# Eleven warm-up matmuls instead of nine ahead of an attention kernel

## The chip, the cores and the metric

The kernel runs on one core of a Trainium2 chip. The metric is the device time of one execution in microseconds (us), as the median of several executions. The profile of an execution also gives its span, from the first to the last instruction; it is 1.7 to 2.0 us shorter than the time. A change counts as faster or slower from 2% on.

## The reference

Two attention blocks read the same x (2048 tokens, 1024 features, bf16, 32 heads of 32) and are mixed by a gate:

```python
g = sigmoid((x * gate_w).sum(-1, keepdims=True))
a = linear_attention(x, A_wqkv) @ A_wo            # phi(q) (phi(k)^T v) / (phi(q) sum phi(k))
b = local_attention(x, B_wqkv, W=8, dil=2) @ B_wo # each token sees 8 keys, two apart
return g * a + (1 - g) * b
```

Nearly all of the work is dense matmuls of 128 x 128 weights on 512 columns.

## The kernel before

The kernel records operations with priorities, and a small list scheduler orders them for each engine. These parts matter here. The zeros of the warm-up, and the warm-up itself, which writes a bank of PSUM (the memory that takes the results of matmuls) that nobody reads:

```python
C("dve", lambda e: e.memset(warm[:, :], 0.0), 0.15, [warm.all()])
for m in mx[0:2]:
    C("dve", lambda e, m=m: e.memset(m[:, :], 0.0), 0.2, [m.all()])
...
for i in range(WARM):
    P.op("pe", lambda e: e.matmul(banks[7].ap(), warm[:, 0:128], warm[:, :], start=True, stop=True), 0.43,
         reads=[warm.all()], writes=[banks[7].iv], prio=-1)
```

The first loads: x tile 0 and half of the first weights in four pieces, then more x tiles, then the other half of the weights, again in four pieces:

```python
load_x(0, 0)                                   # tile, priority
load_w(0, 0, Bw, 2048, 0.1, 0, 2, "act")       # two pieces from the queue of ScalarE
load_w(0, 0, Bw, 2048, 0.2, 2, 4, "act")
load_w(0, 0, Bw, 2048, 0.3, 4, 6)              # two from the queue of SyncE
load_w(0, 0, Bw, 2048, 0.4, 6, 8)
for t in range(1, NT):
    load_x(t, 3 + t)
for d in range(0, 8, 2):
    load_w(0, 1, Bw, 2560, 6.1 + 0.1 * d, d, d + 2)
```

TensorE then works in groups of eight matmuls: x tiles 0 to 3 on the first half of the weights, the same tiles on the second half, then tiles 4 to 7, and so on. The result of a group is then copied out of PSUM by another engine; I call this copy its eviction. Much later in the program, in the last third, a sum over each chunk of 512 tokens is taken by matmuls on `zsel` (L1598 in the profile). This part was not changed, but it comes up below:

```python
for n, (u, j) in enumerate(nums):
    numer(u, j)
    if j == 7:
        after(3, lambda u=u: over(u))     # over(u) issues the L1598 matmuls three slots later
    slot(0)
    ...
```

## Time and profile before

| | before |
|---|---|
| time, median of 3 | 491.82 us (491.49 to 493.79) |
| span of the profiled execution | 492.6 us |
| TensorE busy | 478.7 us, 97% |
| warm-up matmuls | 1.25 to 5.27 us |
| idle until the first tile of x has landed | 1.20 us |
| first real matmul | 6.47 us |

The profiled execution took 494.49 us, longer than each of the three that were timed. The prediction rests on it.

From the page of the profile before: its busy table and its chain of waits (the chain is followed back from the last instruction; shares are of the span).

```profile
PE 478.7 (97%) x5055; PEld 226.9 (46%) x5121; DVE 274.4 (56%) x487; ACT 166.9 (34%) x287; POOL 5.0 (1%) x27
...
PE 91%; DMA 3%; DVE 2%; issue 2%; SPq 1%; ACT 1%; ACTq 0%
```

TensorE (PE) bounds the kernel, so time saved on TensorE reaches the end unless TensorE then waits.

The timeline of TensorE before, first 10 us: start, length, engine, line, operation, tiles, count, and in brackets the idle time ahead of it and what ended that.

```profile
1.25 4.02 PE L1365 MATMUL ps_all<-warm 128*128 128x512 bf16 x9 [1.25 <-DVE warm L1279]
6.47 3.92 PE L1326 MATMUL ps_all<-w,xT 128*128 128x512 bf16 x9 [1.20 <-DMA xT<-in_A_x_dram]
```

Read the lengths: nine warm-up matmuls take 4.02 us and nine real ones 3.92 us, about 440 ns each. Single records start every 427 ns in both rows; from 10.2 us on they start every 216 ns. So the first real matmuls run at half the clock. The trace holds a record of the granted clock as well: full from 10.17 us. (The clock row of the page shows full speed from the start, since it knows nothing before the first record. The spacing of the matmuls is what to trust.)

What TensorE waited for over the whole span before: total us, times, longest.

```profile
PE ps_all L1326 <- issue: 6.0, 38, 0.2
PE ps_all L1365 <- DVE warm L1279: 1.2, 1, 1.2
PE ps_all L1326 <- DMA xT<-in_A_x_dram: 1.2, 1, 1.2
PE ps_all L1598 <- DVE xT L1339: 0.7, 1, 0.7
PE ps_all L1326 <- ACT kT L1358: 0.2, 1, 0.2
```

The 6.0 us of "issue" are holes where the trace lost a matmul record (38 of the 66 that are missing; each hole is one matmul long), not waits.

### The profile page before, as it was taken

What the parts mean: (1) busy time and instruction counts of PE and PEld (TensorE: products, weight loads), DVE (VectorE), ACT (ScalarE), POOL (GpSimd) and SP (SyncE); (2) the same over time, 40 slices, a digit from 0 to 9 for tenths busy, and PEclk for the clock granted to TensorE, in tenths of its full rate; (3) what the DMA queues carried; (4) which work ended last, traced back from release to release, by engine and by line L of the source; (5) the groups of instructions that cost most, each with busy time, mean ns of one, the idle gap of its engine ahead of it and who ended that gap; (6) DMA issues with size and microseconds to landing.
All of it is one profiled execution on the core that took longest, in us unless ns stands there. A gap on an engine that the chain in (4) does not pass through costs nothing.

```text
span 492.6 us, 11357 instructions
## 1 busy us (share of the span) xinstructions
PE 478.7 (97%) x5055; PEld 226.9 (46%) x5121; DVE 274.4 (56%) x487; ACT 166.9 (34%) x287; POOL 5.0 (1%) x27
## 2 busy tenths in 40 slices
PE   8999999999999999999999999999999999999997
PEld 2444444444444444555454454444444444444443
DVE  2121435889777777465555645596865735334434
ACT  1211111222344344665655556355423223010000
POOL 3000000000000000000000000000000000000000
PEclk9999999999999999999999999999999999999999
DMA  8999993232013036201000100501673407101212
GB/s 212 214 201 305 318 358 100 73 95 90 3 27 115 24 116 156 65 26 44 24 24 24 36 12 4 170 3 25 168 191 74 122 11 182 44 23 45 85 67 89
DMA packets 51069, 48.82 MB, mean 99 GB/s; under 512 B 20161, under 2 KB 38977, under 8 KB 51010
## 3 DMA queue, kind: packets, MB, share of 16 engines
q1 hardware_dynamic: 50322, 47.40, 34.6%
q8 instruction: 42, 0.69, 0.6%
q10 hardware_dynamic: 688, 0.59, 0.4%
q14 instruction: 17, 0.14, 0.1%
HBM read 34.34 MB, written 9.44 MB: 89 GB/s over the span
## 4 chain that ended last, share of the span: by engine, by line
PE 91%; DMA 3%; DVE 2%; issue 2%; SPq 1%; ACT 1%; ACTq 0%
PE ps_all L1326 74%; PE ps_all L1647 11%; PE ps_all L1418 2%; PE ps_all L1437 2%; DMA rb<-rc_hbm 1%; DMA xT<-in_A_x_dram 1%; PE ps_all L1519 1%; SPq L1611 1%; PE ps_all L1444 1%; DMA rc_hbm<-ra 1%; DVE zsel L1561 1%; DVE pq L1339 0%; PE ps_all L1598 0%; PE ps_all L1571 0%; DVE e L1337 0%
## 5 line engine op out<-in xcount | busy, mean ns | idle before, releaser
L1326 PE MATMUL ps_all<-w,xT 128*128 128x512 bf16 x921 | 208.5, 381 | 6.1 <-issue 4.3
L1326 PE MATMUL ps_all<-xT,w 128*128 128x512 bf16 x748 | 167.5, 379 | 2.3 <-issue 1.7
L1326 PEld LDWEIGHTS ps_all<-w,xT 128*128 128x128 bf16 x960 | 91.9, 98 | 110.9 <-issue 2.8
L1326 PEld LDWEIGHTS ps_all<-xT,w 128*128 128x128 bf16 x768 | 73.8, 98 | 89.0 <-issue 1.8
L1647 PE MATMUL ps_all<-w,qT 128*128 128x512 bf16 (+1 forms) x259 | 55.3, 372 | 0.3
L1647 PEld LDWEIGHTS ps_all<-w,qT 128*128 128x128 bf16 x264 | 25.8, 98 | 29.7
L1337 DVE TENSOR_SCALAR e<-e 128x512 bf16<-128x512 bf16 x64 | 18.3, 290 | 34.2 <-ACT e L1335 17.0
L1357 DVE CAST vst<-ps_all 128x512 bf16<-128x512 f32 x15 | 10.4, 692 | 45.7 <-PE ps_all L1326 45.7
L1424 ACT ACTIVATE E<-ps_all 128x1824 bf16<-128x1824 f32 (+1 forms) x18 | 30.4, 1687 | 10.1 <-PE ps_all L1418 9.4
L1335 ACT ACTIVATE e<-ps_all 128x512 bf16<-128x512 f32 x32 | 19.1, 597 | 42.8 <-PE ps_all L1326 42.8
L1427 DVE TENSOR_TENSOR E<-E,msk 128x1824 bf16<-128x1824 bf16 (+1 forms) x18 | 19.8, 1102 | 22.4 <-ACT E L1424 22.4
L1651 DVE SCALAR_TENSOR_TENSOR o<-ps_all,gm,xT 128x512 bf16<-128x512 f32 (+1 forms) x25 | 17.9, 728 | 23.3 <-PE ps_all L1647 16.6
L1333 ACT ACTIVATE e<-ps_all 128x512 bf16<-128x512 f32 x32 | 19.1, 597 | 26.6 <-PE ps_all L1326 25.8
L1358 ACT ACTIVATE vst<-ps_all 128x512 bf16<-128x512 f32 x17 | 10.1, 597 | 49.4 <-PE ps_all L1326 49.4
L1287 DVE TENSOR_TENSOR mx<-mx,kT 128x1024 bf16<-128x1024 bf16 x32 | 20.8, 687 | 9.3 <-ACT kT L1358 9.2
L1287 DVE TENSOR_TENSOR mx<-mx,qT 128x1024 bf16<-128x1024 bf16 x32 | 20.8, 686 | 6.8 <-ACT qT L1361 6.7
L1456 DVE TENSOR_TENSOR qT<-ps_all,L 128x456 bf16<-128x456 f32 (+1 forms) x36 | 21.0, 627 | 6.2 <-ACT L L1454 5.0
L1339 DVE SCALAR_TENSOR_TENSOR pk<-ps_all,e 128x512 bf16<-128x512 f32 x32 | 21.9, 688 | 0.7
L1453 ACT ACTIVATE L<-ps_all 128x456 f32<-128x456 f32 (+1 forms) x36 | 17.8, 547 | 12.4 <-PE ps_all L1437 12.4
L1358 ACT ACTIVATE kT<-ps_all 128x512 bf16<-128x512 f32 x16 | 9.6, 597 | 35.8 <-PE ps_all L1326 35.8
L1361 ACT ACTIVATE qT<-ps_all 128x512 bf16<-128x512 f32 x16 | 9.6, 597 | 31.5 <-PE ps_all L1326 31.5
L1614 DVE TENSOR_TENSOR xT<-xT,rb 128x512 bf16<-128x512 bf16 x24 | 16.3, 688 | 7.0 <-DMA rb<-rc_hbm 6.5
(72 smaller groups left out, 284.1 us busy)
## 6 DMA issues: line engine op xcount, KB each, us to landing
rb<-rc_hbm SPq DMA_DIRECT2D x32, 256.0 KB, 4.9
w<-in_A_wqkv_dram SPq DMA_DIRECT2D x6, 1024.0 KB, 8.8
v<-vB_hbm SPq DMA_DIRECT2D x36, 128.0 KB, 2.7
vB_hbm<-vst SPq DMA_DIRECT2D x32, 128.0 KB, 6.0
w<-in_B_wqkv_dram SPq DMA_DIRECT2D x4, 1024.0 KB, 9.2
xn<-in_A_x_dram SPq DMA_DIRECT2D x16, 256.0 KB, 2.7
out_dram<-o SPq DMA_DIRECT2D x15, 256.0 KB, 2.0
w<-in_A_wo_dram SPq DMA_DIRECT2D x8, 256.0 KB, 3.9
```

The lines of the kernel that those rows point to most:

```text
L1287: P.op("dve", lambda e, m=m, op=op: e.tensor_tensor(m[:, 0:n], m[:, 0:n], src, op), 0.08 + n / 1920.0, reads=[m.all(), reg], writes=[m.all()],
L1326: last = e.matmul(bank.ap(), lhs(dc), rhs(dc), start=(dc == 0), stop=(dc == 7))
L1333: P.op("act", lambda e: e.activation(e_[:, :], bank.ap(), ACT.Exp), act(512), reads=[bank.iv], writes=[e_.all()])
L1335: P.op("act", lambda e: e.activation(e_[:, :], bank.ap(), ACT.Exp, accum_out=qe[:, col:col + 1]), act(512) + 0.1, reads=[bank.iv], writes= ...
L1337: P.op("dve", lambda e: e.tensor_scalar(e_[:, :], e_[:, :], 1.0, 1e-6, op0=ALU.min, op1=ALU.add), 0.25, reads=[e_.all()], writes=[e_.all()])
L1339: P.op("dve", lambda e: e.scalar_tensor_tensor(out=dst, in0=bank.ap(), scalar=0.0, in1=e_[:, :], op0=ALU.max, op1=ALU.add), dps(512), read ...
L1358: fa = lambda e: e.activation(dst, src(), ACT.Copy)
L1424: P.op("act", lambda e: e.activation(E[:, 0:32 * nq].rearrange("p (j q) -> p j q", j=4), ps[:, 4:8, 0:8 * nq], ACT.Exp), act(32 * nq), rea ...
L1427: P.op("dve", lambda e: e.tensor_tensor(ev(), ev(), m[:, :, :].rearrange("p r q -> p (r q)")[:, None, :].to_broadcast([128, 16, 2 * nq]), ...
L1456: P.op("dve", lambda e, L=L, h=h, q0=q0: e.tensor_tensor(qT[:, :, q0:q0 + nq], SO[h].ap(0, n).rearrange("p (c q) -> p c q", c=8), L[:, 0:n ...
L1647: last = e.matmul(bank.ap(0, f1 - f0), qT[:, dc, t * 128:(t + 1) * 128], ws[3][:, dc, f0:f1], start=(dc == 0), stop=(dc == 7))
L1651: P.op("dve", lambda e, bank=bank, o_=o_, t=t, n=n, i0=i0, i1=i1, tgt=tgt, c0=c0: e.scalar_tensor_tensor(out=o_[:, i0 * 128:i1 * 128].rear ...
```

## The change

The first tile of x lands at about 6.4 us in this trace, and the nine warm-ups leave TensorE idle for the last 1.2 us. Two more should fill most of it.

```diff
-    WARM = 9
+    WARM = 11
```

A comparison of the two built programs shows the same instructions in the same order with the same waits and buffers on every engine, except for the two added matmuls.

## The prediction

> **What bounds the kernel now.** TensorE. The page's busy table gives PE 478.7 of 492.6 us (97%), and the chain of waits is 91% PE. By the timeline, the nine warm-up matmuls run from 1.25 us (when the zeros are written) to 5.27 us; TensorE then idles 1.20 us until the first tile of x lands, and the real matmuls start at 6.47. In the trace, matmuls start every 427 ns in the warm-up, and still every 427 ns for eight real ones; from about 10.2 us every 216 ns. The record of the granted clock turns full at 10.17 us. So the first 3.7 us of real work ran at half speed, a loss of about 3.7 x (1 - 216/427) = 1.8 us.
>
> **What the change does.** It adds two matmuls of 427 ns each: the warm-up should end near 6.12 us, 0.35 us before x lands. The built program confirms that nothing else moves. The first real matmul should still start at 6.4 to 6.5 us, so the 0.85 us added cost nothing. A gain can come only from the clock.
>
> **What it is worth.** [...]
>
> The 1.8 us can't all be had. Were TensorE fast from 6.47 us, the DMA landings of this trace would hold it: the second x tile lands at 8.64 us where it would be wanted at 8.2, and the last quarter of the weights' second half lands at 15.51 us, wanted at 15.15. Then the fifth group (first x tile, second half) ends near 16.0 us against 16.9 in the trace before: a cap of about 0.9 us against the profiled execution, somewhat more against executions whose clock turned later. After it TensorE is the limit to the end, so what is gained there reaches the end one for one. [...]
>
> **Prediction.** 491.1 us (before 491.82), range 490.1 to 492.3. Faster by over 2%: 0.5%; within 2%: 99%; slower by over 2%: 0.5%.
>
> **What would show each step.** Timeline: eleven warm-ups ending near 6.1 us, idle before the first real matmul 0.3 to 0.4 us, its start unchanged within 0.1. Granted clock: [...]. If early: TensorE waits of about 0.4 us each for the second x tile and the late weights. The three executions before (491.49 to 493.79) already spread by more than the gain; after it the slow ones near 493.8 should be rarer.
>
> **What would make it wrong.** [...] x lands before the warm-up ends, which then delays it by up to 0.4 us. A cause of the spread other than the clock, so that three runs hide the effect.

The sum came to a gain of 0.4 to 1.0 us on average, out of the cap of about 0.9 us, and so from 491.82 to 491.1 us. "If early" means the clock.

## The result, and the profile after

| | before | after |
|---|---|---|
| time in the same rounds, median of 6 | 492.16 us (491.49 to 494.10) | 492.40 us (491.85 to 492.91) |
| span of the profiled execution | 492.6 us | 490.9 us |
| clock full from | 10.17 us | 6.52 us |
| first real matmul | 6.47 us | 6.49 us |

The ratio of the two is 0.9997, with a 95% interval of 0.9974 to 1.002: no difference that can be seen. (A ratio is the mean time of one kernel's runs over that of the other's of the same rounds, so not quite the ratio of the medians in the table. The ratios of the experiments below come out of the record when the first execution of each kernel is left out, so they are not quite the ratio of the means beside them.) Yet the two profiled executions differ by 1.7 us. The same views after, first the page:

```profile
PE 485.7 (99%) x5123; PEld 226.5 (46%) x5123; DVE 274.5 (56%) x487; ACT 166.9 (34%) x287; POOL 5.1 (1%) x27
...
PE 95%; SPq 2%; DVE 2%; DMA 1%; issue 0%
```

Do not read the rise of TensorE's busy time as more real work: of the 68 more matmul records, 66 had been lost before (5055 against 5123) and two are the added warm-ups. The timeline of TensorE after, first 10 us:

```profile
1.25 4.88 PE L1365 MATMUL ps_all<-warm 128*128 128x512 bf16 x11 [1.25 <-DVE warm L1279]
6.49 1.96 PE L1326 MATMUL ps_all<-w,xT 128*128 128x512 bf16 x8 [0.36 <-DMA xT<-in_A_x_dram]
8.71 1.47 PE L1326 MATMUL ps_all<-w,xT 128*128 128x512 bf16 x6 [0.26 <-DMA xT<-in_A_x_dram]
```

The gap shrank from 1.20 to 0.36 us, and eight real matmuls now take 1.96 us: full clock from the first. Then TensorE outruns the loads and waits for the second x tile. All that TensorE waited for after:

```profile
PE ps_all L1365 <- DVE warm L1279: 1.3, 1, 1.3
PE ps_all L1326 <- DMA xT<-in_A_x_dram: 0.6, 2, 0.4
```

The wait at L1598 is absent in this execution. To see where the 1.7 us came from, I set the same evictions of the two traces beside each other in order. The eviction of the fifth group starts at 17.12 us before and 16.09 us after, and the shift stays at 1.03 to 1.08 us until 372 us. Then TensorE and its evictions are 1.73 us apart, to the end. The first part is the clock: 3.7 us less at half speed save 1.8 us, of which about 0.8 come back as waits on loads (the table near the end has the terms). The jump is the wait at L1598. The waits between 364 and 374 us, before:

```profile
DVE xT L1614 <- DMA rb<-rc_hbm: 1.6, 2, 1.3
PEld ps_all L1598 <- DVE xT L1339: 1.2, 1, 1.2
...
PE ps_all L1598 <- DVE xT L1339: 0.7, 1, 0.7
```

and after:

```profile
PEld ps_all L1598 <- DVE xT L1339: 0.5, 1, 0.5
PEld ps_all L1326 <- issue: 0.4, 1, 0.4
DVE xT L1614 <- DMA rb<-rc_hbm: 0.3, 1, 0.3
```

Before, VectorE stood 1.6 us behind a load of `rb`, came late to the product that L1598 reads (L1339), and TensorE waited 0.7 us for it. After, the load came sooner and no matmul waited (the weight load did, for 0.5 us, beside running matmuls). Nothing in the change touches this. So one pair of profiles holds a gain of 1.03 us that may belong to the change and 0.70 us that may be chance, while the means hold nothing at all.

### The profile page after: what moved, and what is told of

Same layout as the page of the kernel before. It is cut to its first block, busy times and chain, and to the rows that moved or that the text cites. A ratio compares the mean times of both kernels' runs of the same rounds, so it can differ in the third digit from the quotient of the medians.

```text
span 490.9 us, 11427 instructions
## 1 busy us (share of the span) xinstructions
PE 485.7 (99%) x5123; PEld 226.5 (46%) x5123; DVE 274.5 (56%) x487; ACT 166.9 (34%) x287; POOL 5.1 (1%) x27
## 4 chain that ended last, share of the span: by engine, by line
PE 95%; SPq 2%; DVE 2%; DMA 1%; issue 0%
PE ps_all L1326 77%; PE ps_all L1647 11%; PE ps_all L1418 2%; PE ps_all L1437 2%; SPq L1300 1%; PE ps_all L1519 1%; DMA w<-in_B_wqkv_dram 1%; PE ps_all L1444 1%; DVE zsel L1561 1%; SPq L1305 1%; PE ps_all L1598 0%; DVE pq L1339 0%; PE ps_all L1571 0%; DVE e L1337 0%; DVE w L1357 0%
## 5 line engine op out<-in xcount | busy, mean ns | idle before, releaser
L1326 PE MATMUL ps_all<-w,xT 128*128 128x512 bf16 x960 | 213.8, 379 | 0.7 <-DMA xT<-in_A_x_dram 0.6
L1326 PE MATMUL ps_all<-xT,w 128*128 128x512 bf16 x768 | 170.7, 379 | 0.0
L1339 DVE SCALAR_TENSOR_TENSOR pk<-ps_all,e 128x512 bf16<-128x512 f32 x32 | 21.9, 688 | 0.7
```

The source lines that it names most:

```text
L1326: last = e.matmul(bank.ap(), lhs(dc), rhs(dc), start=(dc == 0), stop=(dc == 7))
L1339: P.op("dve", lambda e: e.scalar_tensor_tensor(out=dst, in0=bank.ap(), scalar=0.0, in1=e_[:, :], op0=ALU.max, op1=ALU.add), dps(512), read ...
```

## The experiments

**Theories.** The clock theory, a conjecture that these runs test: when the full clock comes depends on how long TensorE stood idle shortly before, so the warm-up changes how often, and how early, the clock turns, and little else. (The last expectations call it the window theory.) The rival: the clock at the start is irrelevant, and the spread between executions comes from waits on DMA, as at L1598.

Two things about the clock the traces do show. The turn is not at a fixed time from the start of the warm-up: in the five traces whose eleven warm-ups all began at 1.25 us it came at 3.99 to 7.18 us. And the record of the full clock lasts 484.693 us in some of the 14 traces (before and after among them), 481.279 and 488.106 us in others. These lengths lie 3.414 and 3.413 us apart, and are 142, 141 and 143 times 3.4133 us. I call 3.413 us the step below.

Spans of all executions are printed in order of size. All outputs are right.

### First four: repeats, no warm-up, and a late warm-up

`nine_again` and `eleven_again` are the two kernels unchanged. `none` has no warm-up:

```diff
-    WARM = 9
+    WARM = 0
```

> The kernel before, unchanged, to get spans of many executions and a second trace. Clock theory[...]: [...]spans without a late stall between 490.9 and 493.3, with two or more clusters. Rival (the clock has nothing to do with it; the spread comes from waits on DMA later in the kernel): the spread is the same as with eleven and the spans don't depend on the warm-up.

> The changed kernel, unchanged, five rounds. Clock theory: [...]spans 490.0 to 491.2, never above 492 unless a late stall shows in the trace; mean 0.5 to 1.0 us below nine_again. Rival: mean within 0.3 us of nine_again, and a spread as wide.

> No warm-up matmul. Clock theory: TensorE starts at about 6.45 us cold, [...]spans average about 1.5 us over eleven_again (492.0 to 493.0). Rival: as nine_again within 0.3 us.

`nine_late` begins the nine warm-ups later, by writing their zeros after two other clears:

```diff
-C("dve", lambda e: e.memset(warm[:, :], 0.0), 0.15, [warm.all()])
 for m in mx[0:2]:
     C("dve", lambda e, m=m: e.memset(m[:, :], 0.0), 0.2, [m.all()])
+C("dve", lambda e: e.memset(warm[:, :], 0.0), 0.15, [warm.all()])
```

> Nine warm-ups, but begun about 1 us later: the zeros are written after two other clears, so that the warm-up ends at 6.1 to 6.4 us and no gap is left before the first real matmul. Clock theory[...]: [...]the mean is within 0.3 us of eleven_again. If it is the number of warm-ups or their early start that counts: as nine_again, clock full at 10 us or later in the trace. Rival: all three kernels within 0.3 us.

| | spans, us | mean | ratio to before |
|---|---|---|---|
| before, same rounds | 490.2 490.2 490.4 490.5 490.8 490.9 491.1 491.2 492.0 492.3 492.5 | 491.1 | |
| nine_again | 490.1 490.5 490.8 490.9 491.1 491.3 | 490.8 | 0.9992 (0.9974 to 1.0010) |
| eleven_again | 490.2 490.3 490.4 490.5 490.7 490.7 | 490.5 | 0.9986 (0.9968 to 1.0004) |
| none | 490.6 490.9 491.0 491.3 491.4 491.6 | 491.1 | 1.0003 (0.9985 to 1.0021) |
| nine_late | 490.3 490.4 490.6 490.9 491.3 491.5 | 490.8 | 0.9995 (0.9976 to 1.0014) |

The traces surprised me twice. The first surprise is `nine_again`, in the timeline of TensorE over the first 14 us:

```profile
1.25 4.02 PE L1365 MATMUL ps_all<-warm 128*128 128x512 bf16 x9 [1.25 <-DVE warm L1279]
5.81 8.38 PE L1326 MATMUL ps_all<-w,xT 128*128 128x512 bf16 x35 [0.54 <-DMA xT<-in_A_x_dram]
```

The x tile landed at 5.76 us here, not at 6.42. The gap is 0.54 us instead of 1.20, and the clock is full from 7.11 us although only nine warm-ups ran. Of the twelve traces that followed the first two, none had x as late as 6.4 us with its issue unmoved. The profile I predicted from was an unlucky one. But the two first traces, of one session, both had x late (6.42 and 6.45 us), so lateness may belong to a session and not to a single execution. No run here decides that.

The second surprise is `none`:

```profile
5.65 8.64 PE L1326 MATMUL ps_all<-w,xT 128*128 128x512 bf16 x33 [5.65 <-DMA xT<-in_A_x_dram]
```

Its clock is full from 8.39 us: without any warm-up, 1.8 us sooner than with nine in the first trace. One step before that is 4.98 us, so TensorE was idle for the first 0.67 us of the last step before the turn. I had expected TensorE to start at 6.45 us; it started at 5.65, since x landed early. The wait at L1598 was 1.0 us in `nine_again`, 0.8 in `eleven_again`, 0.3 in `nine_late` and 0 in `none`: of the order of what the clock does, and in no order with it. It hid the answer, so the next kernels take it away.

Is that wait chance, or does it grow when TensorE runs early? In the seven traces of the original sums the last two loads of `rb` are issued at the same distance from the eighth eviction (to 0.1 us), so their issue just follows TensorE. The last one takes 5.75 and 5.97 us to land in the two traces without a wait, and 6.23 to 6.90 us in the five with one. What varies is how long a load takes. Why it does stays open.

The means missed what I had written down, too. `eleven_again` was 0.3 us below `nine_again`, where the clock theory said 0.5 to 1.0 and the rival at most 0.3; `none` was 0.7 us over `eleven_again`, where the clock theory said 1.5. `nine_late` (clock full from 7.91 us) came out 0.4 us over `eleven_again` where I had expected 0.3 at most; with six executions each this decides nothing. Its trace does show a cost: x landed at 5.73 us, but the late warm-up ended at 6.15, and the first real matmul had to wait for it.

### Second four: without the late wait

Base of these kernels: the sums of the third chunk are issued two groups later, when VectorE is done. With nine, eleven, no and five warm-ups:

```diff
-        after(3, lambda u=u: over(u))
+        after(5 if u == 2 else 3, lambda u=u: over(u))
...
-    WARM = 9
+    WARM = 9      # nine_den5;  11: eleven_den5;  0: none_den5;  5: five_den5
```

> Nine warm-ups; the sums of the third chunk (the matmuls on zsel) are issued two groups later, so that TensorE no longer waits for VectorE near 371 us (0, 0.3, 0.7, 0.8 and 1.0 us in five traces so far). If that wait makes most of the spread between executions: spans fall by about 0.5 us on average against nine_again and the spread shrinks to two clusters: about 490.0 to 490.3[...], and 491.2 to 492.2[...]. If the spread is the clock alone: no fall, and spans still reach 492.5.

> Eleven warm-ups with the same later sums. Clock theory[...]: [...]all spans within 0.3 us of each other, 490.0 to 490.3 when the first x tile lands near 5.8 us (490.9 if it lands near 6.4). If two more warm-ups are worth anything it shows here as the missing upper cluster of nine_den5, a mean 0.2 to 0.6 us lower; if they are worth nothing, equal means within 0.1 us.

> No warm-up, later sums. Clock theory: [...]spans spread evenly from 490.5 to 492.3 us, mean 491.4, about 1.2 us over eleven_den5. If the warm-up does not matter at all: as eleven_den5 within 0.2 us.

> Five warm-ups (1.25 to 3.6 us), later sums. If [...]the gap of over 2 us spoils it: [...]spans as none_den5 within 0.2 us. If warm-up work adds up across a gap[...]: between none_den5 and nine_den5, about half way.

| | spans, us | mean | clock full from (trace) | ratio to before |
|---|---|---|---|---|
| before, same rounds | 490.0 490.4 490.4 490.4 490.7 490.9 490.9 491.1 491.9 492.2 492.4 | 491.0 | | |
| nine_den5 | 489.7 489.8 489.9 489.9 490.0 490.3 | 489.9 | 6.31 us | 0.9980 (0.9963 to 0.9997) |
| eleven_den5 | 489.8 489.8 489.8 490.1 490.3 490.5 | 490.1 | 3.99 us | 0.9980 (0.9962 to 0.9997) |
| five_den5 | 490.7 491.1 491.1 491.7 491.9 492.2 | 491.5 | 10.72 us | 1.0009 (0.9990 to 1.0028) |
| none_den5 | 491.4 491.4 491.6 492.1 492.2 492.3 | 491.8 | 9.70 us | 1.0021 (1.0003 to 1.0039) |

TensorE's waits in `nine_den5`, the whole list:

```profile
PE ps_all L1365 <- DVE warm L1279: 1.3, 1, 1.3
PE ps_all L1326 <- DMA xT<-in_A_x_dram: 0.7, 2, 0.5
```

L1598 is gone from it, the spread is 0.6 us (2.4 in the kernel before, 1.2 in `nine_again`), and the mean falls by 1.0 us against the kernel before, which differs in this edit alone. The second cluster that I had expected never came. Now the warm-up can be read. Against none it is worth 1.8 us with eleven and 1.9 with nine here (0.7 and 0.3 us in the first four); five are worth little (0.4 us better than none, within their spreads), and the gap after them is 2.36 us:

```profile
1.25 2.31 PE L1365 MATMUL ps_all<-warm 128*128 128x512 bf16 x5 [1.25 <-DVE warm L1279]
5.92 8.34 PE L1326 MATMUL ps_all<-w,xT 128*128 128x512 bf16 x27 [2.36 <-DMA xT<-in_A_x_dram]
```

And between nine and eleven there is nothing: 489.9 and 490.1 us. That refutes the rival in its strong form (the warm-up does matter), and, where x lands early, my own size for the change. The six spans of `eleven_den5` lie within 0.7 us, where I had expected 0.3. The faster the clock turns, the more the loads take over: `eleven_den5`, with the full clock from 3.99 us, still waits for x:

```profile
PE ps_all L1326 <- DMA xT<-in_A_x_dram: 1.3, 2, 1.0
PE ps_all L1365 <- DVE warm L1279: 1.3, 1, 1.3
PE ps_all L1598 <- DVE xT L1339: 0.3, 1, 0.3
```

(Its L1598 wait is the second chunk's, at 352 us, which I had not moved.) One thing does not fit: `none_den5` was expected to be faster than `none` and is 0.7 us slower. The two ran in different sessions and on different chips; with six executions each, and the clock's turn known in only one of each (8.39 and 9.70 us), I did not settle it.

### Last four: a late x tile, seven warm-ups, and another repeat

If the clock theory is right, two more warm-ups must count exactly when x lands late. `nine_xlate` and `eleven_xlate` (later sums in both) issue the first x tile after one more piece of the weights:

```diff
-        load_x(0, 0)
+        load_x(0, 0.35)
```

> Nine warm-ups, later sums, and the first x tile issued after one more piece of weights, so that it should land about 0.6 us later (6.3 to 6.5 us), as in the very first trace. Window theory[...]: [...]two clusters, spans near 490.5[...], and 491.3 to 492.2[...]; mean 0.3 to 0.7 us over eleven_xlate. If the length of the gap does not matter: one cluster, equal to eleven_xlate.

> Eleven warm-ups with the same late first x tile. Window theory: the gap is about 0.5 us, [...]one cluster between 490.2 and 490.9 us, none over 491.1. If the two warm-ups are worth nothing even here: as nine_xlate.

`seven_den5` has the later sums and `WARM = 7`:

> Seven warm-ups, later sums, x on time: the gap is about 1.6 us with the landing near 5.8 us. Window theory: [...]mean near 490.9, between nine_den5 (489.9) and none_den5 (491.8). [...]

`eleven_b` is the changed kernel, unchanged:

> The changed kernel a third time, for the shape of its distribution beside that of the kernel before: spans 490.1 to 491.2 as in the twelve so far, while the kernel before shows in about a quarter of its executions spans of 491.9 to 492.5. If such slow executions are chance that has nothing to do with the warm-up, one or two of the six show here too.

| | spans, us | mean | clock full from (trace) | ratio to before |
|---|---|---|---|---|
| before, same rounds | 490.3 490.4 490.4 490.6 490.8 490.9 490.9 491.2 491.8 492.2 492.8 | 491.1 | | |
| nine_xlate | 489.7 489.8 489.9 489.9 491.5 491.8 | 490.4 | 10.19 us (the 491.8) | 0.9981 (0.9961 to 1.0001) |
| eleven_xlate | 489.9 489.9 490.0 490.2 490.2 490.5 | 490.1 | 7.18 us (the 490.2) | 0.9979 (0.9962 to 0.9997) |
| seven_den5 | 490.2 490.3 490.3 490.7 491.0 492.6 | 490.9 | 4.98 us (a 490.3) | 0.9997 (0.9975 to 1.0018) |
| eleven_b | 490.5 490.6 490.9 491.1 491.2 491.4 | 491.0 | 5.40 us | 0.9996 (0.9979 to 1.0014) |

`nine_xlate` falls into two clusters, as the clock theory said: four executions at 489.7 to 489.9 us (I had expected about 490.5) and two at 491.5 and 491.8. The profiled one is of the slow cluster; no trace shows the clock of the fast one, and the two slow ones are the first two. The timeline of TensorE over its first 14 us:

```profile
1.25 4.02 PE L1365 MATMUL ps_all<-warm 128*128 128x512 bf16 x9 [1.25 <-DVE warm L1279]
6.36 7.87 PE L1326 MATMUL ps_all<-w,xT 128*128 128x512 bf16 x27 [1.09 <-DMA xT<-in_A_x_dram]
```

It has nearly the gap of the first trace again (1.09 us for 1.20), and the clock time of the first trace again (10.19 and 10.17 us). The timeline of `eleven_xlate`, with the gap filled:

```profile
1.25 4.87 PE L1365 MATMUL ps_all<-warm 128*128 128x512 bf16 x11 [1.25 <-DVE warm L1279]
6.30 7.93 PE L1326 MATMUL ps_all<-w,xT 128*128 128x512 bf16 x34 [0.17 <-DMA xT<-in_A_x_dram]
```

In the same 7.9 us TensorE starts 34 matmuls instead of 27 (the second trace may lack a record), and all six executions lie within 0.6 us. The means differ by 0.3 us, at the low end of what was expected. `seven_den5` lies between nine and none as expected in the mean; its one execution of 492.6 us is slower than the trace with the longest cold time (`five_den5`, 4.80 us cold, 491.7 us), and I have no trace of it.

`eleven_b` had no slow execution either, as expected if the slow ones come from nine warm-ups (its slowest span is 491.4 us).

`nine_den5`, `eleven_den5` and `eleven_xlate` beat the kernel before by 0.2%, about 1 us. In the last rounds `eleven_xlate` also stands beside the changed kernel: a mean time of 491.99 us against 492.75 for `eleven_b`. In the two traces the gain over that is chiefly the wait at L1598 (0 against 0.8 us), not the clock, which was full by 7.2 us in both.

### What the 14 traces say together

The account below uses the start of the first real matmul, the time when the clock turned, and the cold time between the two (each cold us loses 1 - 215.8/427 = 0.494 us). E8 is the start of the eviction of the eighth group. "DMA waits" are E8 - start - 0.494 x cold - 64 x 0.2158 us: what TensorE lost in its first 64 matmuls beyond the clock; 0.2 of it is in every trace, which I take for the lag of the eviction. "Late wait" is the wait of matmuls at L1598. The rest is the span less E8 less the late wait.

| trace | start | clock full | cold | DMA waits | late wait | span | rest |
|---|---|---|---|---|---|---|---|
| before | 6.47 | 10.17 | 3.70 | 0.20 | 0.7 | 492.6 | 469.6 |
| after | 6.49 | 6.52 | 0.03 | 0.96 | 0 | 490.9 | 469.6 |
| nine_again | 5.81 | 7.11 | 1.30 | 0.56 | 1.0 | 491.3 | 469.4 |
| eleven_again | 5.92 | 6.83 | 0.92 | 0.31 | 0.8 | 490.7 | 469.4 |
| eleven_b | 5.75 | 5.40 | 0 | 0.90 | 0.8 | 490.6 | 469.4 |
| none | 5.65 | 8.39 | 2.75 | 0.20 | 0 | 490.6 | 469.6 |
| nine_late | 6.15 | 7.91 | 1.76 | 0.21 | 0.3 | 490.9 | 469.6 |
| nine_den5 | 5.82 | 6.31 | 0.49 | 0.60 | 0 | 489.9 | 469.5 |
| eleven_den5 | 6.18 | 3.99 | 0 | 0.90 | 0.3 | 490.5 | 469.3 |
| seven_den5 | 5.99 | 4.98 | 0 | 1.11 | 0.1 | 490.3 | 469.3 |
| five_den5 | 5.92 | 10.72 | 4.80 | 0.18 | 0 | 491.7 | 469.5 |
| none_den5 | 5.87 | 9.70 | 3.84 | 0.20 | 0 | 491.4 | 469.6 |
| nine_xlate | 6.36 | 10.19 | 3.83 | 0.20 | 0 | 491.8 | 469.5 |
| eleven_xlate | 6.30 | 7.18 | 0.88 | 0.20 | 0 | 490.2 | 469.5 |

The rest is 469.3 to 469.6 us in every trace, whatever the warm-up. So four numbers account for the spans to within 0.2 us: when x lands, when the clock turns, how long the loads hold a fast TensorE, and the late wait. The clock and the DMA waits trade off: where the clock is full from the start, 0.7 to 0.9 us of the 1.8 us come back as waits.

The table also shows how much TensorE idled before a turn. Take for each trace the step of 3.413 us that ended when the clock turned, and the step before it, and count the idle time from one matmul's start plus its 427 ns to the next. (The profile's modelled ends lie 0.2 us later, so its gaps are 0.2 us shorter: 1.20 us there is 1.40 here.) The step that ended at the turn had at most 0.76 us idle in every trace: 0.67, 0.67, 0.74, 0.75 and 0.76 us in `none`, `eleven_den5`, `nine_again`, `nine_den5` and `seven_den5`, and less in the others. The step before it, at whose end the clock did not turn, had at least 0.90 us idle wherever it lies within the span: 0.90, 0.97, 1.24, 1.25, 1.30 and 1.40 us in `eleven_xlate`, `nine_again`, `eleven_again`, `nine_late`, `nine_xlate` and before, and more in the others. If the idle time in a step is what decides, which is my estimate from these numbers and which no run tests alone, the limit lies between 0.76 and 0.90 us, 22% and 26% of a step. Real data were not needed: in `eleven_den5`, `seven_den5` and `eleven_b` the clock was full at 3.99, 4.98 and 5.40 us, before the first real matmul (6.18, 5.99 and 5.75 us), after matmuls on zeros alone.

With this the change reads plainly. Nine warm-ups end at 5.07 us (last start plus 427 ns); with a gap of up to about 0.8 us, x may land until about 5.9 us and the ninth warm-up is enough. Eleven end at 5.92 us and stretch that to about 6.7 us (both estimates, from the limit above). In the traces with x's issue unmoved it landed between 5.6 and 6.45 us. So I read the change as an insurance for the executions with a late x. In the others it gains nothing and can cost a little: in `eleven_again` x landed at 5.76 us, but the warm-up held TensorE until 5.92.

The distributions lean the same way. Over all rounds, the kernel before ran 45 times (with `nine_again`), the changed one 18 times (after, `eleven_again`, `eleven_b`). Their mean times are 492.80 and 492.47 us, a difference of 0.33 us with a 95% interval of 0.02 to 0.64. Eleven of the 45 are slower than the slowest of the 18 (493.24 us); if the change did nothing, such a split would come up about 1.6 times in 100 (counted over all ways of dealing the 63). But eleven of the 45 are from rounds on a chip where the changed kernel did not run. Round by round the differences are 0.15, 0.54 and 0.19 us, on average 0.29 with a 95% interval of about -0.1 to 0.7 (my working), and the split of the slow ones comes up 2 times in 100.

No trace of those eleven exists. The profiled execution before, as slow as they (494.49 us) but not among the 45, lost 1.8 us to the clock and 0.7 to the late wait. That the eleven have the same cause is not shown. All eleven are among the 39 executions that ran as the kernel before; `nine_again`, the same kernel, had none in six, and `nine_den5` none in six. So a cause that lies in the place of a run within its rounds is not excluded.

## Why the prediction was right or wrong

- *TensorE bounds the kernel; nothing else moves; the added matmuls cost nothing.* Right. The warm-up ended at 6.13 us for 6.12 predicted, the idle time was 0.36 us, and the first real matmul started at 6.49 for 6.47. That holds for x as late as in that trace; the risk that I named, x landing before the warm-up ends, came true in `eleven_again` and cost about 0.15 us.
- *With two more warm-ups the clock turns early.* It did, in all five traces with eleven warm-ups (6.52, 6.83, 5.40, 3.99, 7.18 us). What the traces show is that it turned early with 0.57 us idle in the last step (after; the gap of 0.36 us by the profile), and with up to 0.76 us in others.
- *A cap of about 0.9 us, because TensorE then waits for the second x tile and the last weights, about 0.4 us each.* Right within 0.15 us: the shift was 1.03 us from the fifth group on, with waits of 0.42 us at 8.7 us and 0.26 us at 15.5 us (the spacing of the matmuls there less 216 ns).
- *"After it TensorE is the limit to the end, so what is gained there reaches the end one for one."* Wrong for this pair of profiles. The shift grew from 1.03 to 1.73 us at 372 us. The wait at L1598 stood in my list of waits and I did not ask whether it would be there in the next execution. Five of the seven traces with the original sums have such a wait, of 0.3 to 1.0 us, with nine warm-ups and with eleven; "a cause of the spread other than the clock", which I named as a risk, was real.
- *A gain of 0.4 to 1.0 us on average, 491.1 us.* The direction was right, the size was not: 0.33 us over all executions, and 0.15 us (ratio 0.9997) over the first six executions of each. The step that failed: I gave nine warm-ups much worse odds of an early turn than eleven. That was my estimate, and it took x's landing from a single trace in which it was late. Of the four traces with nine warm-ups and x's issue unmoved, three had the full clock by 8 us (7.11, 7.91, 6.31); only the one predicted from had it late. At the usual landing of 5.6 to 5.9 us the clock turned early after nine as well, and the two kernels are equal (489.9 and 490.1 us without the late wait).
- *The slow executions near 493.8 us should be rarer.* Right in the count: eleven of 45 before, none of 18 after, reach 493.25 us. The cause of those eleven is not shown.
- *The range, 490.1 to 492.3 us.* The measured median of 492.40 us is 0.1 us above it as a plain number, but the kernel before stood at 492.16 us in those rounds and not at 491.82. Scaled by the ratio it is 491.7 us, inside. "Within 2%" was never in doubt. Nor is the number much of a success: the range held the time of the kernel before as well, so it could not tell a small gain from none, and that the number fits owes more to its width than to the 0.4 to 1.0 us behind it.

## What to carry to other kernels

The number of warm-up matmuls did not decide when the clock turned: nine (4.02 us) with a gap of 1.1 to 1.2 us behind them bought nothing in two traces (full clock at 10.17 and 10.19 us, against 8.39 and 9.70 without any), while seven (3.17 us) sufficed in one (4.98 us). What went with the turn in all 14 traces was at most 0.76 us of idle in the 3.413 us before it. So look at the gap: as an estimate from these traces, bridge to the earliest real work with less than about 0.7 us (from the last start plus 427 ns) for the latest landing you see, not for the landing of one trace. Once the clock is full early, ask what the loads will do: here they took back 0.7 to 0.9 of 1.8 us. And before explaining a difference of 1 us between two profiles, line the two traces up event by event: 0.7 of the 1.7 us arose at 372 us, far from the change, from a load that took longer in one execution; taking that wait away was worth more (`nine_den5` against the kernel before in the same rounds: ratio 0.9980, 1.0 us) than the change (0.3 us, hardly clear of noise).
